# 96 matmuls without use in place of 196, at other places of TensorE's order

## The chip, the cores and the metric

One core of one Trainium2 chip. The metric is the device time of one execution of the whole program, in microseconds (us), as the median over runs. TensorE is written PE in the profile (PEld its weight loads), VectorE DVE, ScalarE ACT, GpSimd POOL and SyncE, which issues all transfers, SP.

## What is computed

Two layers, one after the other. The first is attention over 4 batches, 8 heads, 768 positions and 64 channels a head, in which a query sees only those keys that fall in the same bucket. A bucket is the pattern of signs of six random projections. The second mixes the attention's output x (4 x 768 x 512): an angle per element, a product with two 768 x 768 matrices along the positions, and a product with a 512 x 512 matrix.

```python
mask = q_bucket[:, :, :, None] == k_bucket[:, :, None, :]
scores = np.where(mask, scale * np.matmul(q, k.transpose(0, 1, 3, 2)), -1e9)
attn_out = softmax(scores) @ v
theta = x @ w_theta
y = einsum('ts,bsd->btd', w_tok_r, x * cos(theta)) + einsum('ts,bsd->btd', w_tok_i, x * sin(theta))
u = x + y
out = u + maximum(u @ w_ch, 0)
```

## The kernel before

The attention runs in 96 steps (batch, pair of heads, block of 128 queries, two heads a step). A step's work is a fixed sequence. TensorE makes the scores of 128 queries against 768 keys in PSUM (operation `dst` in batch 0, `st` later; tiles `nat`, `hl`, `kb`, `rows`). VectorE takes their maximum (`mc`, L685, or with the mask added L678). ScalarE takes the exponential (`pf`, L698 or L695) and rounds it to 16 bits (`pp`, L704). GpSimd or VectorE makes the remainder (L711). A transposing transfer turns both (`pt`, issued at L715). TensorE multiplies them with the values (`vv`, eighteen matmuls of 64 or 65 columns). When three blocks are through, VectorE divides by the sum (`x`, L765).

Between these steps stands the other work: weights and values are brought in from 64-bit form (`raw`, `wf_th`, `wf_ch`, L240 to L273 and L328 to L357), and the second layer of a batch whose attention is done runs beside the attention of the next (transposes of x at L815, angles, the products with `wtk`). The last batch's second layer stands alone at the end.

All of it is recorded as some 3,500 operations with their dependences. A table, ORDER, gives the order in which they are issued. Each engine gets its instructions in that order and works through them strictly in order; semaphores make it wait where the table's order needs another engine's result. In the table a number is an operation, a digit behind a colon the buffer that it takes, a letter the engine. An entry f0 to f3 is a matmul without use (L148 and L164 to L171):

```python
if x[0] == "f":
    filler(int(x[1:])).alts["PE"][1]()
    continue
...
def go():
    mm(bank(sl, [P, 4, P], "fill"), idle_, idle_.unsqueeze(1).to_broadcast([P, 4, P]), True, True)
```

It loads the constant tile `idle` (128 x 128, 16 bits) as weights and multiplies 512 columns of it into the PSUM bank that the digit names. Nobody reads the result. In the trace these are `ps<-idle`. PSUM has eight banks; scores take six of them, two at a time, and the rest are the small tiles' (`m`, numbers 0 to 3, of which 2 and 3 alone are in use in the first part). A matmul into a bank waits until the bank's last reader is through. All matmuls go through one helper and have line L96, so they are told apart by their tiles.

Of the kernel before, what the change touches and what calls it, by code (L numbers as in the profile page):

```python
# [990 lines left out]
6:0.1 229:0 f2 1 f3 f2 205:0.0 f3 13:0 f2 238:0 f3 7:1 f2 799:0 f3 34:0 f2 373:1 3 f3 2 5D 796:1 236:2 208 234:3 237:0 0 230:2 235 206 232:3 231 f2 233 f2 f3 f2 207 f3 248:0 14 209 239 210G 247:1  # L991
258:0 267:2 211 259 260 249 261:0 240:0 f2 212G f3 f2 250 241 f3 262:0 251 269:1 242 f2 268:0 181:1.0 252:1 264G 243 28 8 253:1 270 263D f3 f2 254G 271 f3 278 265:0 272:2 288:1 255D 273:2 279 280 9
256:1 281:0 310:2 275G 298:2 244:0 287:0 15 282:3 245 f2 376:2 299 274G 289 17 f3 312:0 283G f3 276:2 11 374:3 300 284G 377:1 301:1 290 19 291 182 285:3 292:2 246 f2 f2 f2 311:1 302:0 29 379:0 184 30
304G 293:1 375 331:0 31 321 303G 20:0 10 257:2.0 313 21 314 f3 294G 322 341:1 266 315:0 305:1 22 f3 295G f3 342 316:2 f3 343 323 350:2 12D 296:0 344:1 317D 324:2 35 330:0 378 36 325:3 351:1 183 327G
38 23 f3 f3 332 f3 514:0 32 f3 326G f3 286 352:2 345:0 f3 318G 306 328:3 185 353 333 297 334 347G 354 335:2 277 186D 319:1 346G f3 16 f3 f3 361 f3 336:1 f3 389:0 348:0 362 355:0 363 337G 307 308 338D
187 18G f3 364:1 f3 399:0 f3 f3 408:2 24 400 401 188D 365:3 25 157:1.0 402:2 367G 388:1 40 410:1 49:1 356:2 409:0 366G 380 26 f3 f3 358G 411 403:0 309 368:2 320:3 412 390 349 413:1 357G 517:2 404G
359:1 329 518:0 33G 41:0 391 381:0 515:2 392 419 393:0 339:0 420 37 421 405D 428:2 382 160 406:3 158 394:3 159 27 422:2 395G 429:1 161 516 55:0 423:2 451:0 519 439:2 396G 414:1 383 340 430 162G f2 360
431 440 42 f2 424G 441 397:0 f2 453:0 442:0 f2 369 425D f2 443:0 f2 50 f2 426:1 f2 432 f2 163 454 f2 444G 455 384 f2 433:2 f2 445D 491:1 51 446:2 456:0 416D 385:1 452:2 4 434:3 387 386 f2 43 f2 f2
471:0 462 164G 520:0 463 415D 435G 133:1.0 464 f2 370 465:1 f2 371 473:1 f2 f2 436G 398:2 52 372 407 417:0 39G 474 44 466:2 472:2 475 493:2 476:2 467G 437:3 494 521 457:0 492:0 468G 53 482 f3 458G f3
655:1 483 447 484 56 485:1 f3 f3 469:2 f3 134 f3 427 486:1 135 f3 522:0 477:3 418 487D 488G 438 523 136 495 502 529:2 478G 489:1 496:1 503 448 57 459G 45 530:1 449 47 504 450 656:3 479G 460:0 505:0  # L1000
540:0 54G 531 497:2 480:3 658:2 58 532 533 541 498G 542 534:2 657:1 524 550:0 659 499D 660 46 543:1 549:2 48 506:1 569:1 544:0 551:1 507G 59 461:3 525 546 f2 508D 481 500:0 137 545 490 535:3 552 553
f2 560 f2 554:0 f2 f2 536 547:3 f2 f2 561 526:0 562 f2 571:2 f2 537 470 563:1 f2 509:1 572 138D f2 f2 f2 555:2 60D f2 501 139 538:2 570:2 557 573 528 574:2 527 575:0 61 592:0 556 661:0 580 577 593:1
# [219 lines left out]
```

## Time and profile before

| | us |
|---|---|
| median of 3 runs | 734.14 |
| lowest and highest | 729.14, 736.46 |
| the profiled execution | 729.0 |
| its span, first to last instruction | 727.2 |
| PE busy in it | 714.3 |
| matmuls without use, busy | 59.6 (196 of 379 ns in the median, which overlap) |
| DVE busy | 588.3 |
| ACT busy | 535.4 |

Busy time of PE is the union of its matmuls' times from issue to the last result, so neighbours overlap: the start of the next tells how long one holds the engine. Stretches are named by us from the span's start.

### The profile page before, as it was taken

How to read it: one execution, taken by the hardware profiler on the slowest of the kernel's cores; microseconds unless marked ns; L12 is line 12 of the kernel's file. 1: busy time of each engine (PE TensorE's matmuls, PEld its weight loads, DVE VectorE, ACT ScalarE, POOL GpSimd, SP SyncE). 2: the span in 40 equal slices, each digit the busy share in tenths (PEclk: the TensorE clock that was granted, in tenths of full speed). 3: DMA queues.
4: the chain of work that ended last, by engine and by line, in shares of the span. 5: the costliest groups of instructions: out<-in, count | busy, mean ns of one | idle time of the engine just before them, and what ended most of it. 6: DMA issues, size and time to landing. Idle time of an engine off the chain costs nothing.

```text
span 727.2 us, 17462 instructions
## 1 busy us (share of the span) xinstructions
PE 714.3 (98%) x6644; PEld 468.2 (64%) x6644; DVE 588.3 (81%) x1343; ACT 535.4 (74%) x718; POOL 430.3 (59%) x461
## 2 busy tenths in 40 slices
PE   8999999999999999999999999999999999999998
PEld 3455555566756566787856676777656676884456
DVE  5879986889999999989888886989997887747223
ACT  3786887979999778778998775778986776756000
POOL 4576576776557776976666767556666666611000
PEclk9999999999999999999999999999999999999999
DMA  8899999997786999999867998997769989940002
GB/s 338 178 213 224 198 184 215 177 239 169 172 180 143 195 216 190 231 195 209 167 113 150 205 169 170 184 209 119 135 125 169 168 169 170 167 95 16 1 0 87
DMA packets 324044, 120.97 MB, mean 166 GB/s; under 512 B 306316, under 2 KB 313848, under 8 KB 323960
## 3 DMA queue, kind: packets, MB, share of 16 engines
q1 hardware_dynamic: 323960, 119.86, 82.1%
q8 instruction: 52, 0.85, 0.5%
q14 instruction: 32, 0.26, 0.1%
HBM read 32.56 MB, written 6.29 MB: 53 GB/s over the span
## 4 chain that ended last, share of the span: by engine, by line
PE 69%; DVE 11%; DMA 8%; ACT 7%; issue 3%; POOL 1%; SPq 0%; DVEq 0%; ACTq 0%; POOLq 0%
PE ps L96 67%; DMA pt<-pp 6%; DVE pf L678 3%; PE ps L815 2%; ACT pp L704 2%; ACT pf L695 2%; DVE mk L674 1%; POOL pp L711 1%; DVE l_x L824 1%; DMA raw<-in_wt_dram 1%; ACT pf L698 1%; DVE f L893 1%; DVE raw L331 1%; DVE vv L404 1%; ACT n L856 1%
## 5 line engine op out<-in xcount | busy, mean ns | idle before, releaser
L711 POOL TENSOR_TENSOR pp<-pf,pp 128x384 f16<-128x384 f32 x372 | 347.1, 957 | 186.5 <-ACT pp L704 141.5
L96 PE MATMUL ps<-z,wtk 128*128 128x512 f16 x864 | 203.2, 379 | 0.4 <-DVE rows L536 0.4
L695 ACT ACTIVATE pf<-pf,mc 128x768 f32<-128x768 f32 x144 | 133.3, 930 | 53.5 <-DVE mc L681 41.5
L704 ACT ACTIVATE pp<-pf 128x768 f16<-128x768 f32 x192 | 159.7, 838 | 15.4 <-DMA pt<-pp 12.9
L678 DVE CUSTOM_DVE_ANT_1 pf<-ps,mk 128x768 f32<-128x768 f32 x144 | 136.6, 952 | 31.7 <-POOL pp L711 15.1
L96 PEld LDWEIGHTS <-pt 128*128 128x128 f16 x3456 | 120.4, 97 | 27.7 <-issue 6.9
L96 PEld LDWEIGHTS <-wtk 128*128 128x128 f16 x864 | 78.6, 98 | 87.4 <-issue 4.0
L96 PE MATMUL ps<-vv,pt 128*128 128x65 f16 (+1 forms) x3456 | 129.5, 193 | 1.0 <-DVE x L933 0.4
L96 PE MATMUL ps<-hl 64*128 64x512 f32 (+1 forms) x864 | 97.7, 352 | 1.3 <-DVE mc L678 1.3
L96 PEld LDWEIGHTS ps<-hl 64*128 64x128 f32 x864 | 73.2, 184 | 27.8 <-issue 9.4
L674 DVE TENSOR_SCALAR mk<-kb,qc 128x768 bf16<-128x768 bf16 x144 | 85.1, 604 | 0.3
L96 PE MATMUL ps<-nat 64*128 64x512 f32 (+1 forms) x192 | 71.0, 506 | 0.3 <-ACT pf L698 0.2
L96 PE MATMUL ps<-wth,h_x 128*128 128x512 f32 x192 | 65.2, 420 | 0.2 <-DVE l_x L824 0.2
L96 PE MATMUL ps<-wch,h_u 128*128 128x512 f32 (+1 forms) x200 | 64.4, 405 | 0.0
L698 ACT ACTIVATE pf<-ps,mc 128x768 f32<-128x768 f32 x48 | 46.9, 985 | 22.5 <-DVE mc L691 16.0
L96 PE MATMUL ps<-idle 128*128 128x512 f16 x196 | 59.6, 391 | 3.4 <-DVE l_x L824 1.2
L904 POOL TENSOR_TENSOR z<-f,z 128x512 f16<-128x512 f32 x25 | 32.3, 1295 | 47.1 <-ACT z L898 34.7
L685 DVE TENSOR_REDUCE mc<-ps 128x1 f32<-128x768 f32 x48 | 45.1, 948 | 11.6 <-PE ps L96 10.5
L820 ACT ACTIVATE h_u<-ps 128x512 fp32r<-128x512 f32 x24 | 14.2, 591 | 50.0 <-PE ps L815 33.8
L96 PEld LDWEIGHTS ps<-nat 64*128 64x128 f32 x192 | 28.8, 186 | 25.9 <-issue 17.9
L893 DVE SCALAR_TENSOR_TENSOR f<-x,zsc,z 128x512 f32<-128x512 f32 x48 | 37.4, 798 | 4.4 <-ACT z L882 2.7
L96 PEld LDWEIGHTS ps<-wch,h_u 128*128 128x128 f32 x200 | 35.7, 188 | 7.8 <-ACT rows L543 0.3
(125 smaller groups left out, 961.5 us busy)
## 6 DMA issues: line engine op xcount, KB each, us to landing
nat<-in_qk_dram SPq DMA_DIRECT2D x32, 384.0 KB, 3.9
raw<-in_wt_dram SPq DMA_DIRECT2D x12, 768.0 KB, 5.1
vb<-in_v_dram SPq DMA_DIRECT2D x16, 384.0 KB, 4.2
out_dram<-x SPq DMA_DIRECT2D x23, 256.0 KB, 2.8
kb<-rows SPq DMA_DIRECT2D x48, 96.0 KB, 2.6
pt<-pp SPq DMA_TRANSPOSE x192, 4.2
w_th<-in_moe_w_theta_dram SPq DMA_DIRECT2D x4, 512.0 KB, 5.5
w_ch<-in_moe_w_ch_dram SPq DMA_DIRECT2D x8, 256.0 KB, 4.0
```

The costliest lines, as they stand in the source:

```text
L96: PE.matmul(out_, l, r, start=start, stop=stop, skip_group_check=True)
L674: DVE.tensor_scalar(u["mk"][:, :, : S // 3], t["code"][:, j].rearrange("p (a n) -> p a n", a=3), t["qc"][:, i, j : j + 1], -APART, ALU.not ...
L678: DVE.tensor_tensor_reduce(u["pf"].rearrange("p (a n) -> p a n", a=3), st[j].rearrange("p (a n) -> p a n", a=3), u["mk"][:, :, : S // 3], ...
L685: DVE.tensor_reduce(col(0), st[j], AX.X, ALU.max, negate=True)
L695: ACT.activation(u["pf"], u["pf"], AF.Exp, bias=col(2), scale=1.0 / math.sqrt(D))
L698: ACT.activation(u["pf"], st[j], AF.Exp, bias=col(2), scale=col(1))
L704: ACT.activation(u["pp"][:, 0], u["pf"], AF.Copy)
L711: return lambda: eng.tensor_tensor(u["pp"][:, 1, cols], u["pf"][:, cols], u["pp"][:, 0, cols], ALU.subtract)
L815: PE.transpose(u["pt"][:, c], src()[:, c * P : (c + 1) * P], ident)
L820: ACT.activation(u["hi"], u["pt"], AF.Copy)
L893: DVE.scalar_tensor_tensor(u["f"], tl[b][:, tt], zsc[:, b : b + 1], t["zw"][r][:, tt], ALU.mult, ALU.mult)
L904: return lambda: eng.tensor_tensor(t["z"][r, 1][:, tt], u["f"], t["z"][r, 0][:, tt], ALU.subtract)
```

## The change

The table alone is changed. Its 3,518 operations stay, with the same order, buffers and engines. Of the 196 f entries 96 are left, and most of these stand elsewhere: 196 in 160 places (a place is a run of f entries without another between), the longest of eight, against 96 in 34 places, the longest of fifteen. By bank f0 to f3 they were 26, 28, 75 and 67, and are 0, 31, 36 and 29. The first ten, in front of the first useful matmul, are the same. By the useful work that they stand beside, with the stretches in which the trace of before has that work:

| stretch, us | 0:9 | 9:62 | 62:75 | 75:150 | 150:224 | 224:260 | 260:727 |
|---|---|---|---|---|---|---|---|
| before | 10 | 41 | 19 | 61 | 52 | 5 | 9 |
| after | 10 | 24 | 2 | 44 | 15 | 1 | 0 |

(One of before lies across 62 us and counts in both columns.) The first line of the table:

```diff
-6:0.1 229:0 f2 1 f3 f2 205:0.0 f3 13:0 f2 238:0 f3 7:1 f2 799:0 f3 34:0 f2 373:1 3 f3 2 5D 796:1 236:2 208 234:3 237:0 0 230:2 235 206 232:3 231 f2 233 f2 f3 f2 207 f3 248:0 14 209 239 210G 247:1
+6:0.1 229:0 f2 1 f3 f2 205:0.0 f3 13:0 f2 238:0 f3 7:1 f2 799:0 f3 34:0 f2 373:1 3 f3 2 5D 796:1 236:2 208 234:3 237:0 0 230:2 235 206 232:3 231 233 207 248:0 14 209 239 210G 247:1 258:0 267:2 211 259
...
```

VectorE's, ScalarE's, GpSimd's and SyncE's instructions stand in the same order as before, with the same waits.

PE, beside the first batch's second block of scores, near 16 us: `row`, `ones` and `vam` belong to the scale of the values, `nat`, `kb` and `rows` to the scores. Before:

```order
L96 LDWEIGHTS row_104
L96 MATMUL ps<-ones,row_104 128x1
L96 LDWEIGHTS idle
L96 MATMUL ps<-idle 128x512
L96 MATMUL ps<-nat_0_116 128x512
L96 LDWEIGHTS rows_88
L96 MATMUL ps<-kb_90,rows_88 128x512
```

After:

```order
L96 LDWEIGHTS idle
L96 MATMUL ps<-idle 128x512
L297 MATMUL ps<-ident,vam_0_170 1x128
L96 LDWEIGHTS row_104
L96 MATMUL ps<-ones,row_104 128x1
L96 MATMUL ps<-nat_0_116 128x512
L96 LDWEIGHTS rows_88
L96 MATMUL ps<-kb_90,rows_88 128x512
```

The matmul without use between `ones` and the scores is gone. A run of three, whose last is shown, stands in front of the transpose of `vam` now; before, a run of four stood behind that transpose.

PE, at the first angles of batch 0, near 153 to 156 us: `ident,x` are transposes of the attention's output, `hl` scores of batch 1, `wth` with `h_x` and `l_x` the angles. Before:

```order
L96 MATMUL ps<-hl_0_1458 128x512 x6
L96 MATMUL ps<-hl_0_1458 128x256 x6
L96 LDWEIGHTS idle
L96 MATMUL ps<-idle 128x512
L96 MATMUL ps<-wth_96,h_x_0_2080 128x512
L96 MATMUL ps<-wth_97,h_x_0_2080 128x512
L96 MATMUL ps<-wth_96,l_x_0_2081 128x512
L815 MATMUL ps<-ident,x_597 128x128 x4
L96 LDWEIGHTS idle
L96 MATMUL ps<-idle 128x512
L815 MATMUL ps<-ident,x_597 128x128 x4
```

After:

```order
L96 MATMUL ps<-hl_0_1420 128x512 x6
L96 MATMUL ps<-hl_0_1420 128x256 x6
L96 MATMUL ps<-wth_96,h_x_0_2024 128x512
L96 MATMUL ps<-wth_97,h_x_0_2024 128x512
L96 MATMUL ps<-wth_96,l_x_0_2025 128x512
L815 MATMUL ps<-ident,x_580 128x128 x8
```

The matmuls without use between the scores, the angles and the transposes are gone, so that two groups of four transposes follow each other at once.

## Rows read from the trace of the kernel before

**Rows 1.** The page: engines' busy time and share; granted clock by slice; the chain by engine.
```profile
PE 714.3 (98%) x6644; PEld 468.2 (64%) x6644; DVE 588.3 (81%) x1343; ACT 535.4 (74%) x718; POOL 430.3 (59%) x461
...
PEclk9999999999999999999999999999999999999999
...
PE 69%; DVE 11%; DMA 8%; ACT 7%; issue 3%; POOL 1%; SPq 0%; DVEq 0%; ACTq 0%; POOLq 0%
```

**Rows 2.** Windows: start and end, length, busy us (and instructions) by engine, clock, DMA.
```profile
9.00:62.00 53.00, 51.92 (x359) 26.31 (x358) 44.38 (x96) 40.66 (x54) 30.56 (x29) 1.00 0.96 235
62.00:75.00 13.00, 13.00 (x119) 7.09 (x115) 12.71 (x33) 8.85 (x11) 8.47 (x9) 1.00 1.02 234
75.00:150.00 75.00, 74.09 (x744) 43.07 (x743) 62.23 (x143) 63.19 (x82) 51.77 (x56) 1.00 0.98 195
150.00:224.00 74.00, 71.32 (x668) 47.13 (x665) 70.38 (x156) 69.76 (x95) 46.30 (x46) 1.00 0.87 184
224.00:260.00 36.00, 35.20 (x332) 20.95 (x334) 32.91 (x80) 28.11 (x44) 27.58 (x32) 1.00 0.91 181
260.00:727.20 467.20, 461.60 (x4420) 320.82 (x4419) 362.57 (x830) 322.81 (x432) 261.29 (x280) 1.00 0.77 146
```

**Rows 3.** Chain that ended last, by line, of 9:62, 75:150, 150:224, 224:260, 260:727 us.
```profile
by line: PE ps L96 94.6%; ACT pf L698 1.9%; DVE kb L495 1.5%; PE ps L297 1.2%; issue 0.8%; DVE ones L301 0.5%; DVE mc L691 0.3%; ACTq L698 0.0%
...
by line: PE ps L96 72.7%; DMA pt<-pp 15.7%; ACT pf L698 5.2%; DVE mc L685 2.6%; issue 2.0%; PE ps L297 1.0%; ACT pp L704 0.9%; DVE ones L301 0.4%; DVE mc L688 0.3%; ACTq L704 0.0%; DVE mc L691 0.0%; POOL pp L711 0.0%; ACTq L698 0.0%; ACTq L
...
by line: PE ps L96 22.4%; DVE pf L678 11.2%; issue 8.0%; DVE mk L674 7.3%; DMA raw<-in_wt_dram 6.9%; DVE f L893 6.0%; DVE z L904 3.9%; DVE l_x L824 3.6%; DVE raw L331 3.0%; DVE raw L328 2.7%; DVE vv L404 2.6%; DVE qt L578 2.5%; DVE x L765 2
...
by line: PE ps L96 47.9%; DMA pt<-pp 16.8%; ACT pf L695 10.1%; ACT pp L704 6.8%; issue 4.5%; ACT hl L449 4.3%; DVE pf L678 2.5%; POOL pp L711 2.4%; DVE x L933 2.1%; ACT wf_ch L249 1.8%; ACT wf_ch L250 0.8%; ACT wch L270 0.5%; DVE mc L678 0.
...
by line: PE ps L96 74.1%; DMA pt<-pp 6.3%; PE ps L815 3.1%; DVE pf L678 2.4%; issue 2.3%; ACT pp L704 2.0%; ACT pf L695 1.6%; POOL pp L711 1.1%; DVE mk L674 0.7%; ACT n L856 0.7%; DVE l_x L824 0.6%; ACT L695 0.5%; ACT h_x L820 0.5%; DVE z L
```

**Rows 4.** Windows of the tile idle alone: the matmuls without use.
```profile
9.00:62.00 53.00, 11.25 (x41) 3.25 (x40) 0.00 (x0) 1.00 0.96 235
62.00:75.00 13.00, 5.03 (x19) 1.46 (x18) 0.00 (x0) 1.00 1.02 234
75.00:150.00 75.00, 17.47 (x61) 4.93 (x62) 0.00 (x0) 1.00 0.98 195
150.00:224.00 74.00, 17.00 (x52) 4.41 (x52) 0.00 (x0) 1.00 0.87 184
224.00:260.00 36.00, 1.56 (x5) 0.42 (x5) 0.00 (x0) 1.00 0.91 181
260.00:727.20 467.20, 3.25 (x9) 0.87 (x9) 0.00 (x0) 1.00 0.77 146
```

**Rows 5.** Timeline of PE near 1, 10 and 64 us: start, length, instruction, idle before.
```profile
1.12 4.07 PE L96 MATMUL ps<-idle 128*128 128x512 f16 x10 [1.12 <-DVE idle L80]
...
9.96 0.81 PE L96 MATMUL ps<-idle 128*128 128x512 f16 x3 [0.27 <-DVE kb L495]
...
63.88 1.89 PE L96 MATMUL ps<-idle 128*128 128x512 f16 x8
```

**Rows 6.** DVE's waits, 9:62 us (three), then 75:150 (two): total, times, longest.
```profile
DVE mc L685 <- PE ps L96: 3.3, 4, 1.8
DVE rows L478 <- PE ps L96: 1.7, 1, 1.7
DVE ones L301 <- PE ps L96: 1.2, 1, 1.2
...
DVE mc L685 <- PE ps L96: 7.2, 8, 2.7
DVE ones L301 <- PE ps L96: 1.4, 1, 1.4
```

**Rows 7.** Timeline of PE near 150 us.
```profile
150.65 0.82 PE L96 MATMUL ps<-idle 128*128 128x512 f16 x3
...
152.72 0.33 PE L815 MATMUL ps<-ident,x 128*128 128x128 f32 x1 [0.92 <-DVE x L765]
```

More of the change, by code (lines that the diff above doesn't have):

```diff
@@ new lines @@
+345:0 318G 306 328:3 185 353 333 297 334 347G 354 335:2 277 186D 319:1 346G 16 361 336:1 f3 f3 f3 f3 389:0 348:0 362 355:0 363 337G 307 308 338D 187 18G 364:1 399:0 f3 f3 408:2 24 400 401 188D 365:3
+25 157:1.0 402:2 367G 388:1 40 410:1 49:1 356:2 f3 f3 f3 409:0 366G 380 26 358G 411 403:0 309 368:2 320:3 412 390 349 413:1 357G 517:2 404G 359:1 329 518:0 33G 41:0 391 381:0 515:2 392 419 393:0 339:0
+420 37 421 405D 428:2 382 160 406:3 158 394:3 159 27 422:2 395G 429:1 161 516 55:0 423:2 451:0 519 439:2 396G 414:1 383 f2 340 430 162G 360 431 440 42 424G 441 397:0 453:0 442:0 369 425D 443:0 50
@@ new lines @@
+568 635 619 636 610:1 637:2 671:1 69 800 621:2 798D 647:3 801G 670:0 666 638:2 66 672:0 640 588 625 681 626:0 639 682 602:3 673 589 627:0 3515:2 3516 70:0 674 590 67 641:0 802:0 675:2 629 683 f1 f1
+622 2572:0.0 667:1 76:1 628 676:1 591 f1 f1 f1 f1 f1 f1 f1 691:0 649 630:3 684:0 677 f1 f1 690:1 648 701:2 678 650:2 642 702 692 668 807:1 693 703 694 2573 704:1 679:0 669 808:0 71 f2 f2 f2 f2 f2
+710:0 685:2 77 815:0 72 803 687 695:2 611 712:1 705:0 631 686 696:3 713 733:1 714 2574 688:1 715:0 78 698 74 809 804 f2 711:0 80 697 735:0 79 707 699:3 651 736 737 721 680:2 738:2 706 82 810:1 722
@@ new lines @@
+716:1 723 81D 734:1 708:2 724:1 717 816 811 812:0 718 725:2 753:0 744 73 727 944:1 83:0 689 745 84 719:0 739:3 746 2575 726 755:2 747:0 805:0 f1 f1 f1 817:0 740 728:1 818 85 756 748:0 754:1 757 86 75D
+758:1 749 806 947:0 773:0 87 764 814 741 89 700 765 766 750 775:1 767:2 709 88 768:1 751:3 f1 f1 774:1 90 759:2 770 776 742:2 720 784 945:1 769 729 652 91:0 946G 730 785 731 819 777 786 771:0 813
+787:0 732 778:2 761 834:0 2579:1 820 2580:0 760 824:1.0 97:1 788:0 2581 779:3 825:1 790 653 2582:0 826:0.1 821:0 789 2589:2 844:1 2599:1 781 827 835:0 2583 828 780 654 2584 948 836 92 2585 782:1
@@ new lines @@
+2590:1 949G 853:0 2586:0 843:1.0 2591 829:1 2587 837 93 743:3 830 2600:0 762:2 845:2.2 772 95 2592:2 831 846 872:1 847 791:0 98 2593 94 2576 99 2594 848:3 2595 823 101 850 752 854:1 963:0 783 100
+1095:1 2588D 822 763 2596:1 103 849 855 2601 856 2597 2602:0 96D 857:2 862:1.0 2598A 863:0 859 838:0 964 858 2639 2603 873:1.2 839 860:3 104:0 874 864:1 792 840 f1 f1 f1 f1 f1 f1 f1 f1 f1 f1 f1 f1 f1
+f1 f1 965:0 851:1 865 793 102G 894:1 2604 794 105 866 2605 795 2640:2 841:2 2609:1 2643:0 106 884:0.1 2641D 2606:1 832:0 107 2642G 867:2 885:0 950:2 2607 2644A 868 2610:1 886:0.0 2629:3 951:1 2645G
@@ new lines @@
+919 2723 934 2636:0 882 883 918 2724 2663A 2637 2725 122 920:0 2659:0 1093:0 972:1.0 2655D 2660A 971 911:1 927:0 893:3 2664D 935 929 124 1111:0 961 902 936:1 2678:0 982:1 928 973:0 2628A 2679 937
+983:0.2 115 930:2 2702 1096 2680 938 974:1 2703 2638A 984 117D 985 2681 1094D 991:0.1 121 2661D 986:2 1240:0 2682 992:1 939:3 2665 987 1001:0 125:0 2704 1112 988 2683 1002:2.0 2726 123G 921 975 1003
+993:2 2684 976 970 1097D 1010:1.0 2669:2 1243:1 2705 2666:1 989:0 977:3 931 2672:0 912 978 126 2673A 1042:0 127 940 2667A 994 1011:1 979 1113:0 2727 2670A 941 2674D 1004 2706 2671G 942 2685 943 1005:0
@@ new lines @@
+1054 154D 1055 1070:1.0 1119 1056:2 166 1063 2745 167 155 1071:0 1057 168 2746 2734 1259:0 1241:1 1028 1058 1109 1064 2747 1072:1.2 156G 1059:1 169 1065:3 2748 1073 1081:1 170G 2749 1074 1118 173:1.2
+1067 1082 1120:1.0 1130:0 1075:0 1049:2 1121:1 1066 1083 2766:2 1076 1131:0.0 171 1068:0 2750 1084:2 1077 1132 2767 1029 1140:0 1244 172G 2751 1122:2 176 1041:1 1086 1123 1149:1 2768 1124 1078:3 174
+2752 175 1125:1 1242D 1139:0.1 1133 189:0.1 1030 1126 1031 1391:0 2753 1260 1134:3 1127 177 1069 1085 1150:2.2 f3 1261:0 2754 1136 1087:0 1141:1 2755 1079 1135 1142 1151 1159:1 1143 1158:1.0 1128:3
@@ new lines @@
+1168:0 178G 1245D 2769 179 192 190 1050 1144:0 2577 180D 1060 191 1152 1262 1146 2770 197:2.0 2756 193 1246:3 1137:2 1169:1.0 1145 1153:2 1088 1247:1 1160:1 1154 1263 1251:0 1388:1 1181:0 1155 2771
+1252 1161 1200:1 1180:0.1 1162 194G 1156:1 1248 198 1163:1 1170 1253 2772 1182:0.2 195 1147:0 1165 2773 1171 199 1129:3 1164 1172:3 1089 2774 1264 1183 1190:0 1254:0 1138 1174 1166:3 1255 1090 1191:1
+2775 1184 1173 2776 1091 1265:1 196D 1249:0 1175:2 1199:0.1 1192 1185:2 1267 200 1186 1193 2788:1 213:1.2 1201:2.0 2789 1256:1 1250 1187 201 1202 2790 1209:0 1194:0 2791 202D 1258 1203 1210:2 1196
@@ new lines @@
+2713:0 1157 1219:1 2714:1 1195 1218:0.1 1211 1204:1 2715 1212 2578 1188:1 1205 1176 1220:1.1 1389:0 2777 1206 1213:3 1257 1197:2 1167 2691:0 214 203 215 2792 2692:0 1228:0 204G 2793 216 1278:1 217
+1214 221:0.1 2794 1221 1229:0 1222 1207:3 1148 1215 1230 1269:0 1223:2 1268:0.1 1177 1178 1231 218D 1216:0 1224 1179 2795 1392 1279:0.2 1225 1232:0 1189:3 1270:1 2796 219 1226:1 1234 2797 1271 222
+1233 1272 1287:1.0 1288:1 1280 1297:0 1273:1 223 1198 1281 1289:2.0 1275 2798 1235:2 2693 1208 1282:3 1274 1217 1316:1 224 1283 2799 225 1407:0 1298:1 2735:0 1276:3 226G 1299 1306:1.0 2778 1300 1284
@@ new lines @@
+1290 2800 227 220G 1301:2 1227 1307:0 1285:0 228D 1291 1236 1303 1317:1.2 2716:2 1292:0 1237 1266 2810:0.0 1302 2694:1 1390G 2695 1338:1 2696 1308:1 2697 1408 1294 1539:1 1328:0.1 1304:1 1238 1293
+1318 1309 2698 1310 1329:0 1409:0 1393G 2717 1319 2699 1330:0.0 2718 1311:1 1410 2719 1331 1239 2736:0 1536:0 1312 1394:1 1295:2 1332 2737 1277:3 1313 2720 1320:3 1399:0 1348:0 2721 1395:0 1322 1339:1
+2757:2 1333:2 1314:3 1305 1321 1400 1357:1 1347:0.1 2758:1 1396 1335 1323:1 1340 2759 1341 2738:1 1334 1401 1358:2.2 1397:2 1342:0 1404:0 1411 1402:0 1286 1398 1349:0 1344 2739 1403 1406 1412 2740
@@ new lines @@
+1523 1532 2887D 2889:2 2888G 2913 1696 1587 1697 2858 1533 2896D 2890A 2933:0 1588:2 2891G 1603:1 2934 1534 2859:0 2935 1596 1590 2860 2936 1535 1578:3 2937 1589 2861D 1698:2 1597:0 1580 1591:1 2955:3
+1604:1.1 1699 2914 2898 1599 1605 2938 1706 2892:2 1693:2 1579 2915 1612:0 2956 2916 1598 1581:3 1613:2 2957 2893A 1606 1614 1624:1.0 2908:0 1600:2 2894D 2897D 2958 2905:2 1707 1832:1 2959 1607:1
+2902:1 2939 1694 1609 1625:1 2903A 2960 1615 2904D 2940 1608 2917 1634:0 1616:2 1626:0.0 2918 2906A 1618 1573:2 1627 1635:1 1592 1617 1610:0 1601 1636 2899:1 1637 2961 2962 1619:1 2900A 1638:3
@@ new lines @@
+2031 3020 3051 2016:3 2039 2130D 2032:3 3065:2 2040 1967 2056:0 2033 2046:0.1 2047:1 2132 2034 2152 2041:1 3057 1948 2023 2057:1.2 3052:1 1976 3066:1 2042 2025:1 3058:3 2058 1977 2069:0 2153:1 2133G
+3059 1978 2048:1 2059 3060 1979 3061 3067 2043 2068:1.0 2078:1 3062:0 2049 2044:2 3053 2060:0 3054D 3075:0 2070:0.0 2061 2017:2.1 3076:0 2035:0 3068:1 2050 3063 2062 3069 2071 2051:2 2079:2 2276:0
+3070 2072 2063:3 2052 3077 3071 2080 2097:0 3085:3 2081 2053 2087:1.0 2088:1 3072:2 2155 3086:1 3078:0 3064D 2073:1 3087 3079 3105 2089:2.1 2075 3088:3 3073 2074 3080 2107:1 3081 3074D 2090 3095:1
@@ new lines @@
+2036 3096:0 3106:1 3089 3082:0 2054:0 3107D 2091 3090 3083 3108G 3097 3091 3112:2 2134:0 3115:0 3113A 2026 2135:1 3084D 2139:1 3114G 2098:0 3116A 2064 2092:3 3109:1 2055 2140 2093 2045 2082:0 2136
+2106:1.0 3092:2 2065 2141 2083 2116:0 3118 2144:1 3110D 2142:0 2094 3098:1 3093 2076:1 3099 2066 2084 2117:1.1 3100 3111G 2108:2 2085:3 3101 3094A 2099 3125:2 2137:3 3117G 2156:0.1 2138 2279:1 2118
+2109 2143 3119:1 2110 2146 3188:3 3166:0 3120D 3167 2067 2119 3122:0 3168 2095:0 3144:2 3121D 3123A 3126D 3189 2111:2 3124G 3127D 3169 2120:1 3145 3102:1 2122 3190 2145 2100 3191 3103 2121 2101:0 3170
```

116 lines of the change are left out of this document (36 added, 80 removed), and 50 rows, old and new, of the table ORDER.

## Prediction

> **What bounds the kernel now.** I read the page's engine shares first. TensorE is busy for 98% of the span, VectorE for 81%, ScalarE for 74%, and the chain that ended last lies on TensorE for 69%; the granted clock is full in every slice [rows 1]. That looks like a kernel bound by TensorE, but part of its busy time is matmuls that nobody reads, so I cut the span into stretches and asked for the engines and for the useless matmuls ("idle" ones from here on) in each.
>
> The table by stretch shows two kinds of time [rows 2]. From 62 to 75 us VectorE is busy 12.71 of 13 us, and from 150 to 224 us 70.38 of 74: there VectorE sets the pace. From 9 to 62 us it is busy 44.38 of 53 and from 75 to 150 us 62.23 of 75, while TensorE is busy 51.92 and 74.09. The chain by stretch agrees: TensorE's matmuls hold 94.6% of it from 9 to 62 us, 72.7% from 75 to 150, only 22.4% from 150 to 224, then 47.9%, and 74.1% (with 3.1% for transposes) from 260 us to the end [rows 3].
>
> The Trainium skill, page Perfetto Trace Analysis, section Identifying the Most-Contended Engine, says that the matmul row's busy share is a poor measure and that for TensorE the weight loads' busy share should be compared with the other engines' occupancy. Loads are busy 64%, VectorE 81% [rows 1], so by that rule VectorE is the contended engine, idle matmuls cost nothing, and the sum would be 0. The chain by stretch speaks against it for two of the early stretches and the long last one [rows 3].
>
> **The change, part by part.** On the other four engines nothing moves, and TensorE's useful matmuls keep their order. What changes is how many idle ones stand before each of them. Their number by stretch is 41, 19, 61, 52, 5 and 9 [rows 4]; in the new order, placed beside the same work, 24, 2, 44, 15, 1 and 0. The first ten, before 9 us, stay.
>
> Price of one: a run of eight lasts 1.89 us and a run of three 0.81, so five more cost 1.08, or 0.216 us each [rows 5]. That is what an in-order engine loses when useful work stands ready behind it. Where useful work would have waited anyway, it costs nothing.
>
> From 9 to 62 us: 41 out, 24 in, 17 fewer at 0.216: 3.7 us. TensorE holds the chain, as at the scores near 16 us, where the idle matmul in front of them goes, so I count all of it. This also takes the 24 that stay at full price, as if none stood in a wait; against that, some waits that idle matmuls fill today come back bare. TensorE's idle time in this stretch is 53 less 51.92, or 1.1 us, and I leave that as it is. Bounds: nothing, if each removed one only uncovers a wait; at best what VectorE waits for TensorE here, for it can't be faster than without those waits: 3.3, 1.7 and 1.2 us in the largest rows, 6.2 in all [rows 6].
>
> From 62 to 75 us: 19 out, 2 in. VectorE has 0.3 us to give, so 0; this is the cover for the 17 removed.
>
> From 75 to 150 us: 61 out, 44 in, 17 fewer: 3.7 us. Bounds: nothing, and the waits of VectorE for TensorE, 7.2 and 1.4, together 8.6 [rows 6].
>
> From 150 to 224 us: 52 out, 15 in, the 15 in a single run before one transpose. 37 at 0.216 would be 8.0 us of TensorE's time, but VectorE is idle for only 3.6 us of the stretch [rows 2]. I count 0, since the chain has TensorE at under a quarter here; at best the 3.6. Those between the scores and the angles near 154 us are among them. What is late next is VectorE itself: one idle run of three ends as the transposes begin, and the last of these waits 0.92 us more for VectorE's result (its multiply at L765) [rows 7]. With the run taken out, that wait is longer by the run and nothing else changes.
>
> From 224 to 260 us: 4 fewer are 0.9 us, of which the chain's share, 47.9%, is 0.4. After 260 us 9 go: 1.9 us, and 77.2% of the chain is TensorE's: 1.5. Bounds: nothing, and 0.9 and 1.9.
>
> Idle matmuls write other banks now. One of those removed waited for its bank: of the run of three at 9.96 us the first stood 0.27 us for VectorE's read of the projected bits [rows 5]. The new ones stand in banks whose last reader is further back in the order, and I expect no such wait: 0, at worst the same 0.27 us in each of the 25 places behind 9 us (6.8 us), at best the same 0.27 gained. Nothing on another engine waits for an idle matmul, so no queue is held up but TensorE's own. The DMA queue's issues keep their order; they come earlier with the work that they wait for.
>
> Sum: 3.7 + 0 + 3.7 + 0 + 0.4 + 1.5 = 9.3 us off the profiled execution's 729.0 us (a span of 727.2 and 1.8 around it), so 719.7. The median of the three runs, 734.1, stands 5.1 above the profiled one; I carry the difference over to it: 724.8 us.
>
> **The clock.** The first ten idle matmuls take 4.07 us, nearly twice the price above [rows 5]: at the start TensorE runs at the lower of its two levels, 1.2 GHz. After that the clock is at 2.4 GHz in every stretch [rows 2], and the engine is never idle long: the whole table has it idle 2.7 us between 150 and 224 us, the stretch where it waits most. No row of before shows the clock falling in the middle, so its price has to be bounded: half speed costs half a microsecond of work per microsecond. The Trainium skill, page TensorE: Matmul & The Clock Gate, section Why this matters for your kernels, says that idle time between bursts of matmuls brings the clock down to half. This trace neither contradicts nor shows that, since its gaps are filled; it speaks against a change that opens them. What it would make of the time is the third rival's price.
>
> **The rivals.**
> First, the same again under another name: the removed matmuls stood where the engine has to wait, so each stretch keeps its length, and only the last two terms remain: 1.9 us, 732.2. For it: ScalarE and VectorE are busy 63 and 62 of 75 us themselves [rows 2], and scores may only start when ScalarE has emptied their banks, so a TensorE that is ahead soon stands. Against it: in two stretches VectorE waits for TensorE, 14.8 us in the rows shown [rows 6]. Anything under 7.3 us, 1% and about what a measurement can tell here, counts in this case.
>
> Second, better than forecast: the 68 idle matmuls left between 9 and 62 and between 75 and 150 us stand in real waits and cost nothing. Then the two stretches give all that VectorE waits for, 14.8, and the end 1.9: 16.7 us, 717.4. Against it: other waits of VectorE's (for ScalarE, for a transfer) come up long before the last of these is gone.
>
> Third, slower: the clock falls between 150 and 224 us, where the new order has one run of 15 and nothing else in place of 52 spread out. TensorE's useful work there is 71.3 less 11.2 (52 at 0.216), 60.1, with the 15 63.3 us, so it has 10.7 us to spare. Each microsecond at half speed takes half a microsecond of that. It decides from 40 of the 74 us on: 20 us lost, 10.7 spare and 9.3 gained elsewhere. At 57 us it loses 28.5, and the kernel ends 8.5 us late: 742.6. For it: the bare gap at the transposes alone is 0.92 us and the run of three before it [rows 7], and there are many like it. Against it: an engine at half speed has no gaps left, and at the start it took steady work to bring the clock up, so it should come back.
>
> That the change does not do what it says can only mean that the waits it was placed by are not those of this chip; then the first rival's time holds.
>
> **How the numbers follow.** Forecast, faster by 7.3 to 14 us: 0.36. Second rival: 0.16. So faster by over 1%: 0.52. First rival, within 1%: 0.33. Third, slower by over 1%: 0.15. Time: 724.8. The range starts at 715, which takes in the second rival, and ends at 738, short of the third rival's price; together about 2 in 10 lie outside.
>
> **What would show it.** Right: idle matmuls number 96; VectorE's waits for TensorE between 9 and 150 us fall to about half; the work that now starts at 150 us starts some 7 us earlier, and the work of 224 us keeps that lead without adding to it; the granted clock stays full. First rival: TensorE's idle time before 150 us grows by as much as the idle matmuls shrink. Third: the clock row falls below full between 150 and 260 us. The forecast is wrong if the lead at 150 us is under 4 us, if the stretch with VectorE at its limit gets shorter by more than 3.6, or if the lead is lost after 260 us.

## The result and the profile after

The changed kernel takes 735.35 us in the median of 22 runs (730.84 to 742.27), the kernel before, beside it, 730.45 (22 runs): a ratio of 1.0055, with an interval of 1.0041 to 1.0069. It is half a per cent slower, where 724.8 us and 9.3 us off had been predicted. Its profiled execution takes 734.41 us, 5.4 more than the one of before (729.0).

The page of the kernel after, busy time by engine and granted clock by slice:

```profile
PE 708.5 (97%) x6544; PEld 466.1 (64%) x6544; DVE 588.0 (80%) x1343; ACT 535.4 (73%) x718; POOL 427.6 (58%) x461
...
PEclk9999899999999999999999999999999999999999
```

TensorE is busy 5.8 us less than before [rows 1], and still the span is 5.4 us longer. One slice of the clock row is below full: 73 to 92 us. Windows of the kernel after, with the columns of [rows 2] (start and end, length, busy us by engine, granted clock, DMA):

```profile
9.00:62.00 53.00, 51.84 (x385) 27.25 (x385) 48.75 (x110) 43.53 (x58) 32.27 (x33) 1.00 1.02 254
62.00:75.00 13.00, 11.04 (x62) 5.16 (x61) 12.72 (x28) 9.08 (x13) 8.06 (x7) 0.82 0.95 214
75.00:150.00 75.00, 71.53 (x668) 41.56 (x668) 54.85 (x131) 56.73 (x74) 46.19 (x50) 0.96 0.89 180
150.00:224.00 74.00, 66.37 (x605) 45.00 (x603) 68.27 (x149) 67.75 (x91) 44.88 (x45) 0.95 0.82 179
224.00:260.00 36.00, 35.55 (x354) 21.62 (x352) 33.69 (x82) 31.45 (x49) 26.81 (x29) 1.00 0.85 176
```

By 62 us VectorE has done 4.4 us more work than before (48.75 against 44.38). From 62 us on the mean clock is 0.82, 0.96 and 0.95, and between 75 and 150 us VectorE, ScalarE and GpSimd all do 5 to 8 us less than in [rows 2]. Something between 62 and 150 us takes away what the first stretch won.

VectorE's waits for TensorE in the kernel after, 9 to 62 us (two rows), then 75 to 150 us, as in [rows 6]:

```profile
DVE rows L478 <- PE ps L96: 1.8, 1, 1.8
DVE mc L685 <- PE ps L96: 0.5, 1, 0.5
...
DVE mc L685 <- PE ps L96: 8.1, 7, 3.3
DVE ones L301 <- PE ps L297: 3.6, 3, 2.6
DVE rc L755 <- PE ps L96: 1.7, 2, 1.3
DVE ones L301 <- PE ps L96: 1.4, 1, 1.4
```

From 9 to 62 us the 6.2 us of waits have become 2.3. From 75 to 150 us they have grown: the two rows named before make 9.5 us in place of 8.6, the row for L297, 0.9 us before, makes 3.6, and the row at L755 is new.

The place where the first gain turns into a loss is in TensorE's timeline near 70 us. First the kernel after, then before (start, length, instruction, idle before in brackets):

```profile
66.09 1.27 PE L96 MATMUL ps<-vv,pt 128*128 128x65 f16 x36
69.31 1.20 PE L96 MATMUL ps<-nat 64*128 64x512 f32 x2 [1.96 <-ACT pf L698]
...
84.55 2.79 PE L96 MATMUL ps<-nat,pjs 128*56 128x512 f32 x8
```

```profile
71.25 1.04 PE L96 MATMUL ps<-idle 128*128 128x512 f16 x4
72.12 1.25 PE L96 MATMUL ps<-vv,pt 128*128 128x65 f16 x36
73.31 1.12 PE L96 MATMUL ps<-nat 64*128 64x512 f32 x2
...
83.87 2.79 PE L96 MATMUL ps<-nat,pjs 128*56 128x512 f32 x8
```

The same thirty-six matmuls start 6.0 us earlier (66.09 against 72.12), the scores behind them 4.0 earlier (69.31 against 73.31): they stand idle for 1.96 us until ScalarE's exponential has emptied their banks. At the next landmark, the product `nat,pjs`, the kernel after is 0.7 us late (84.55 against 83.87). So 4.7 us go in these 15. Windows of the kernel after, around that wait and at a later fall of the clock:

```profile
67.36:69.31 1.95, 0.00 (x0) 0.00 (x0) 1.92 (x6) 1.04 (x2) 1.95 (x2) 1.00 0.97 330
69.31:70.24 0.93, 0.93 (x2) 0.39 (x3) 0.86 (x5) 0.93 (x2) 0.07 (x1) 1.00 1.10 348
70.24:80.48 10.24, 10.24 (x85) 6.43 (x84) 6.80 (x16) 7.34 (x11) 7.41 (x8) 0.50 0.69 165
80.48:90.00 9.52, 9.52 (x39) 4.38 (x36) 7.09 (x16) 6.05 (x8) 1.49 (x2) 1.00 0.80 150
172.64:176.05 3.41, 3.41 (x16) 2.41 (x15) 3.19 (x6) 3.38 (x5) 2.71 (x4) 0.50 0.11 39
```

TensorE does nothing from 67.36 to 69.31 us, works on, and 0.93 us later its clock falls to the lower level, 1.2 GHz, for 10.24 us. It is busy throughout them, so they hold 5.1 us of work at 2.4 GHz, and 5.1 us are lost, close to the 4.7 above. The clock falls again for 3.41 us at 172.64 us, behind 2.36 us in which the angles wait for VectorE, and for 3.41 at 217.01, behind 1.48 us. It did not fall behind every such wait: the transposes near 154 us now wait 2.12 us, and the clock stays full.

```profile
156.67 0.33 PE L815 MATMUL ps<-ident,x 128*128 128x128 f32 x1 [2.12 <-DVE x L765]
```

From here on a kernel's lead is how much earlier the same instruction of VectorE ends than in before's profile, or of TensorE where rows of TensorE are shown. VectorE's instructions stand in the same order in every kernel here, so they are matched by their place in it, and a lead "at 108 us" is that of the instruction that ends at 108 us in before's profile. Some expectations below name leads that differ from these, by almost 3 us near 91 us and by up to about 1 us elsewhere. Before's profile is of one of its faster executions (729.0 us against a median of 730.45), so the leads are on the low side.

In the kernel after the lead is +3.7 us from 60 to 79 us, -0.7 from 85 to 97, -3.2 at 108, -4.4 at 126, -3.7 at 174, -5.9 at 180 and -5.4 at the end. The first drop is that of the clock at 70 us. Part of the second stands near 103 us. Timeline of the kernel after, then of before:

```profile
103.16 0.27 PE L297 MATMUL ps<-ident,wmx 128*1 128x128 f32 x1
103.27 1.89 PE L96 MATMUL ps<-idle 128*128 128x512 f16 x8
105.00 0.71 PE L96 MATMUL ps<-vv,pt 128*128 128x65 f16 x18
```

```profile
101.05 0.27 PE L297 MATMUL ps<-ident,wmx 128*1 128x128 f32 x1
101.28 0.72 PE L96 MATMUL ps<-vv,pt 128*128 128x65 f16 x18
```

A new run of eight idle matmuls stands before eighteen matmuls, which in before start at once. TensorE's lag of 2.1 us becomes 3.7. The third drop, from -2.8 us at 120 to -4.4 at 126, comes at a run of seven. The fourth, 2.2 us at 178, stands behind the run of fifteen. TensorE's timeline of the kernel after, then of before:

```profile
176.10 0.71 PE L96 MATMUL ps<-vv,pt 128*128 128x65 f16 x18
176.66 3.40 PE L96 MATMUL ps<-idle 128*128 128x512 f16 x15
179.89 0.27 PE L297 MATMUL ps<-ident,vam 128*1 128x128 f32 x1
```

```profile
172.61 0.71 PE L96 MATMUL ps<-vv,pt 128*128 128x65 f16 x18
173.16 0.27 PE L297 MATMUL ps<-ident,vam 128*1 128x128 f32 x1
```

TensorE's lag of 3.5 us ahead of the fifteen is 6.7 behind them. VectorE's next read of a product from behind them (L219), in the kernel after, then in before:

```profile
183.41 0.16 DVE L219 TENSOR_SCALAR winv<-ps 128x1 f32<-128x1 f32 x1 [2.79 <-PE ps L96]
```

```profile
177.54 0.16 DVE L219 TENSOR_SCALAR winv<-ps 128x1 f32<-128x1 f32 x1 [0.62 <-PE ps L96]
```

VectorE waits 2.79 us there in place of 0.62, which is the whole drop of 2.2. The two falls of the clock in this stretch cost next to nothing: across the one at 172.64 us the lead goes from -3.5 to -3.7, and across the one at 217.01 it stays at -5.4.

### The profile page after: what moved, and what is told of

Read it like the earlier page. It is cut to its first block, busy times and chain, and to the rows that moved or that the text cites. A ratio compares the mean times of both kernels' runs of the same rounds, so it can differ in the third digit from the quotient of the medians.

```text
span 732.6 us, 17267 instructions
## 1 busy us (share of the span) xinstructions
PE 708.5 (97%) x6544; PEld 466.1 (64%) x6544; DVE 588.0 (80%) x1343; ACT 535.4 (73%) x718; POOL 427.6 (58%) x461
## 5 line engine op out<-in xcount | busy, mean ns | idle before, releaser
L96 PEld LDWEIGHTS <-wtk 128*128 128x128 f16 x864 | 78.5, 98 | 88.1 <-issue 5.5
L96 PE MATMUL ps<-hl 64*128 64x512 f32 (+1 forms) x864 | 100.6, 356 | 2.9 <-DVE mc L678 2.8
L96 PEld LDWEIGHTS ps<-hl 64*128 64x128 f32 x864 | 75.2, 187 | 29.8 <-issue 8.9
L96 PE MATMUL ps<-nat 64*128 64x512 f32 (+1 forms) x192 | 77.4, 517 | 2.8 <-ACT pf L698 2.7
L96 PEld LDWEIGHTS ps<-nat 64*128 64x128 f32 x192 | 31.2, 190 | 32.1 <-issue 17.6
L96 PE MATMUL ps<-wth,l_x 128*128 128x512 f32 x96 | 38.4, 400 | 2.4 <-DVE l_x L824 2.4
```

What stands on the lines that cost most here:

```text
L96: PE.matmul(out_, l, r, start=start, stop=stop, skip_group_check=True)
```

## The experiments

All are the table alone. In the diffs only the part of a line around an edit stands. "Clock" is the granted clock over a whole execution; a fall of 10.24 us makes it 0.993, and one of 3.41 us 0.998.

**First: the nineteen of 62 to 75 us put back (after with before's idle matmuls there, 113 in all).**

```diff
-397:0 453:0 442:0 369 425D 443:0 50 426:1 432 163 454 444G
+397:0 f2 453:0 442:0 f2 369 425D f2 443:0 f2 50 f2 426:1 f2 432 f2 163 454 f2 444G
...
```

> The changed order with the 19 idle matmuls of before put back between 62 and 75 us (113 in all). Theory A (the clock's fall at 70 us, 10.2 us at half speed, took some 5 us): no fall there, the lead of about 4 us at 62 us is still there at 85 us, time some 4.7 us under the changed kernel, near 730.7. Theory B (removal buys nothing, the lead would be lost to other waits and to idle matmuls in front of ready work): lead gone by 108 us either way, time near 735.

Measured: 736.72 us, ratio 1.0056 (1.0026 to 1.0086). The fall at 70 us is gone, and the lead is +3.3 us from 85 to 97 us, where the kernel after has -0.7. But the kernel is no faster, against the first theory's 730.7: the lead runs into the next wait. Timeline of this kernel, then its windows from there on:

```profile
90.91 0.81 PE L96 MATMUL ps<-idle 128*128 128x512 f16 x3
93.33 0.72 PE L96 MATMUL ps<-vv,pt 128*128 128x65 f16 x18 [1.61 <-DMA pt<-pp]
```

```profile
94.36:108.01 13.65, 13.65 (x47) 5.83 (x46) 3.24 (x5) 4.55 (x6) 7.10 (x9) 0.50 0.57 119
```

It waits 1.61 us for a transfer, and the clock is at 1.2 GHz for 13.65 us after it. The lead is +3.3 us at 97, -5.9 at 103 and -5.7 at 108. In this execution the fall had only moved to the next place where a lead ends in a bare wait.

**Second: the fifty-two of 150 to 224 us put back (133).** The run of fifteen goes, and the scattered ones return.

```diff
-864:1 792 840 f1 f1 f1 f1 f1 f1 f1 f1 f1 f1 f1 f1 f1 f1 f1 965:0 851:1 865 793
+864:1 792 840 965:0 f2 851:1 865 f1 793
...
```

> The changed order with the 52 idle matmuls of before in place of the 15 between 150 and 224 us (133 in all). Theory A: the fall at 70 us stays, the two of 3.4 us at 172 and 217 us go, time 1.5 to 3.4 us under the changed kernel, 732 to 734. Theory B: VectorE sets the pace there, so no difference, 735.

Measured: 732.87 us, ratio 1.0012 (0.9989 to 1.0034). In its profile the fall at 70.24 us is still there (10.24 us), the two at 172 and 217 are gone, and the lead is -4.1 at 174 and at 180 us, where the kernel after drops from -3.7 to -5.9; VectorE's wait at L219 is 0.63 us. By the ratios (1.0055 less 1.0012) the late stretch of the change costs 0.43%, or 3.1 us. This run takes the fifteen and the two falls away together; that it is the fifteen, for 2.2 us of it, is read from the profile of the kernel after.

**Third: the new places of 9 to 62 us alone, all else as before (180).**

```diff
-270 263D f3 f2 254G 271 f3 278 265:0 272:2 288:1 255D 273:2 279 280 9 256:1 281:0 310:2
+270 263D 254G 271 278 265:0 272:2 288:1 255D 273:2 279 280 9 256:1 281:0 f2 f2 f2 f2 f2 310:2
...
```

> The order of before with the new 24 in place of 40 idle matmuls between 9 and 62 us, all others as before (180 in all). Theory A: the clock stays full, the 3.7 us of lead that the changed kernel has at 62 us are kept to the end, time 3 to 4 us under before, near 727. Theory B: the lead at 62 us is the same 3.7, but is absorbed by 150 us, time as before, near 730.5.

Measured: 730.06 us, ratio 0.9981 (0.9958 to 1.0005). The lead is +3.9 us at 60 and still +3.3 at 132: the term of the first stretch, to within half a microsecond. Then it goes at once. Timeline and window of this kernel:

```profile
130.85 1.87 PE L96 MATMUL ps<-nat 64*128 64x512 f32 x2 [1.80 <-ACT pf L698]
```

```profile
131.09:137.92 6.83, 6.83 (x47) 3.52 (x46) 3.31 (x6) 4.85 (x8) 4.98 (x5) 0.50 0.56 113
```

The scores stand 1.80 us for ScalarE, the clock falls 0.24 us later, and the lead at 139 us is -1.6. By time the ten executions do not differ by their clock: six with 0.998 or more have a mean of 730.8 us, four with 0.995 to 0.997 have 730.5.

**Fourth: both of the first two together (150).** The edit is the two diffs above.

> The changed order with the idle matmuls of before between 62 and 75 us (19) and between 150 and 224 us (52), 150 in all. Theory A: clock full everywhere, time 6 to 8 us under the changed kernel, 727 to 729, under before. Theory B: near 735, or 733 if the falls cost something.

Measured: 731.66 us, ratio 0.9998 (0.9974 to 1.0023). Up to 94 us its profile is that of the first experiment, down to the wait:

```profile
93.35 0.72 PE L96 MATMUL ps<-vv,pt 128*128 128x65 f16 x18 [1.60 <-DMA pt<-pp]
```

```profile
94.36:108.01 13.65, 13.59 (x119) 7.50 (x118) 8.79 (x25) 9.43 (x12) 9.21 (x12) 1.00 0.92 185
```

Yet the clock doesn't fall: 119 matmuls in the 13.65 us that held 47. So the wait alone does not decide, and one kernel's executions differ. Of this kernel's ten, six have a clock of 0.998 or more and a mean of 730.7 us, four have 0.993 and 734.8: in this kernel a fall goes with 4.1 us. In the profiles the fall is worth more: at 103 us the lead is +0.6 here and -5.9 in the first experiment. With the clock full the lead is still lost, though later: +3.3 at 97 us, +0.6 at 103, +1.2 at 120, -0.4 at 126. At these two places the runs of eight and of seven stand, which the change brought.

**Fifth: the third, with eight idle matmuls in the wait near 130 us (188).** The eight write into a bank that a small product is in (f3), so that this product's value is changed.

```diff
-78 698 74 809 804 711:0 80 697 735:0 f2 f1 79
+78 698 74 809 804 f3 f3 f3 f3 f3 f3 f3 f3 711:0 80 697 735:0 f2 f1 79
```

> e3 with eight idle matmuls more in front of the scores at 129 us, where TensorE stood bare for 1.8 us before the clock fell (188 in all). If the bare wait is what lets the clock fall: clock full, the lead of 3.3 us shrinks at that wait to some 1.5 to 2 (ScalarE's time there) but isn't lost, time 1 to 2 us under before, 729. If the fall comes from something else: it stays at 131 us, with 5 us lost as in e3, 730.

Measured: 729.50 us, ratio 0.9979 (0.9961 to 0.9996). The scores follow the eight at 131.44 us, and the same window is at full clock:

```profile
129.61 1.90 PE L96 MATMUL ps<-idle 128*128 128x512 f16 x8
131.44 1.12 PE L96 MATMUL ps<-nat 64*128 64x512 f32 x2
```

```profile
131.09:137.92 6.83, 6.83 (x60) 3.70 (x58) 3.85 (x8) 6.83 (x13) 5.31 (x7) 1.00 0.98 202
```

All ten executions have 0.998 or more, against six of ten without the eight. But the time is the same (0.9979 against 0.9981): the lead of +2.7 us at 132 is +1.0 at 139 and -0.9 at 168. The eight are more than the wait needs, since the scores start 0.6 us later than in the third (131.44 against 130.85). ScalarE is busy for all 6.83 us of that window; here the lead is spent on the other engines, whatever the clock. The first rival, that a lead is absorbed, is right for this version.

**Sixth: the fourth without the runs of eight and of seven (135).**

```diff
-576 62:0 f2 f2 f2 f2 f2 f2 f2 f2 510 603
+576 62:0 510 603
...
-676:1 591 f1 f1 f1 f1 f1 f1 f1 691:0 649
+676:1 591 691:0 649
```

> e4 without the run of eight idle matmuls at 103 us and the run of seven near 121 us (135 in all). If these two stand in front of work that is ready: the lead of 4.2 us at 102 us is kept to 115 us in place of 1.0, and time is 2 to 3 us under e4, 728 to 729. If they stand in waits: the lead is the same 1 us at 108 us, with bare waits there and perhaps a fall of the clock, 731.7 or more.

Measured: 730.48 us, ratio 0.9964 (0.9932 to 0.9996), and wide: 725.93 to 737.17. Five executions with a clock of 0.998 or more have a mean of 727.4 us, 3.3 less than the fourth's six at that clock (before's own means at that clock, beside the two, differ by 0.2): that is what the two runs cost. Three with 0.993 have 731.7, and two with 0.986 took 734.25 and 737.17. The profiled one, of 0.993, has a fall of 10.24 us at 95.27, again behind the wait for the transfer (1.64 us).

**Seventh: before without its last fourteen (after 224 us, with the single one of the change; 183).**

```diff
-1047 f0 2712 f0 2744:0 1110
+1047 2712 2744:0 1110
...
```

> The order of before without the last 14 idle matmuls but the one of the changed order near 257 us (183 in all). By the terms of the prediction 0.4 and 1.5: 1.9 us under before, 728.5 to 729.5. If the work behind most of them waited anyway: no difference, 731.

Measured: 732.09 us, ratio 1.0003 (0.9980 to 1.0027). The lead stays within 1 us of zero up to 600 us and is -1.5 at the end. No gain is to be seen: the 1.9 us of the two terms would be 0.9974, below the interval.

**Eighth: only the first ten left (10).**

```diff
-231 f2 233 f2 f3 f2 207 f3 248:0
+231 233 207 248:0
...
```

> No idle matmul but the first ten. If bare waits let the clock fall: several falls between 20 and 260 us, more time at half speed than the 17 us of the changed kernel, time over 737. If the idle matmuls only cost: 5 to 10 us under before, 722 to 726.

Measured: 745.37 us, ratio 1.0148 (1.0084 to 1.0213). The page's clock row of this kernel:

```profile
PEclk9679889568999999999999999999999999999999
```

Eight falls, 78.5 us before 232 us. The first, at 16.42 us, comes behind idle times of only 0.59 and 0.37 us. The lead at the end is -19.2.

**Ninth: the sixth, with the run of three near 91 us made ten (142).**

```diff
-138D 555:2 60D f2 f2 f2 501 139
+138D 555:2 60D f2 f2 f2 f2 f2 f2 f2 f2 f2 f2 501 139
```

> e6 with the run of three idle matmuls near 91 us made ten (142 in all), so that the bare wait of 1.6 us behind it, after which the clock fell in e6, is filled. If the fall took the lead (6.0 us at 91 us, -2.2 at 108): clock full, the lead is about 4 us at 97 us and still 3 to 4 at 108, time 3 to 4 us under before, 727 to 728. If not: the lead at 108 us is 0 or less and time is that of before.

Measured: 727.62 us, ratio 0.9934 (0.9911 to 0.9957): below both kernels. Five of six executions have 0.998 or more (727.4 us). The ten now fill the wait for the transfer:

```profile
90.85 2.32 PE L96 MATMUL ps<-idle 128*128 128x512 f16 x10
93.30 0.72 PE L96 MATMUL ps<-vv,pt 128*128 128x65 f16 x18
```

The eighteen start at 93.30 us with the ten as at 93.51 with three. The profiled execution, the sixth, took 734.12: its clock fell later, behind a bare wait of 0.89 us, and its lead went from +2.2 at 134 us to -3.5 at 142.

```profile
132.00:145.65 13.65, 13.28 (x80) 7.44 (x79) 6.24 (x16) 8.74 (x13) 8.09 (x10) 0.50 0.72 147
```

**Tenth: before with the run of eight of 103 us added (204).**

```diff
-576 f2 62:0 510 603
+576 f2 62:0 f2 f2 f2 f2 f2 f2 f2 f2 510 603
```

> The order of before with one run of eight idle matmuls added where the changed order has its run of eight, in front of a product with the values near 101 us (204 in all). If that product is ready there: TensorE is 8 times 0.216, 1.7 us late at once, and up to 1.7 us of it reach the end: 732 to 733.5 beside 731.5. If it waits there: nothing, 731.5.

Measured: 733.99 us, ratio 1.0027 (1.0007 to 1.0047); the clock of the profiled execution is full. Its timeline, to be read beside the two at 103 us above:

```profile
101.26 0.27 PE L297 MATMUL ps<-ident,wmx 128*1 128x128 f32 x1
101.37 1.89 PE L96 MATMUL ps<-idle 128*128 128x512 f16 x8
103.09 0.71 PE L96 MATMUL ps<-vv,pt 128*128 128x65 f16 x18
```

The eighteen start 1.8 us later than in before. Of these 1.3 arrive (lead -0.2, then -1.5 at 108 us), and they stay to the end. (The table of before has no run of more than three; where TensorE's timeline of before shows eight in a row, entries of other engines stand between them.) The run stands before ready work.

**Eleventh: the ninth, with the one near 130 us made five (146).**

```diff
-78 698 74 809 804 f2 711:0 80 697
+78 698 74 809 804 f2 f2 f2 f2 f2 711:0 80 697
```

> The last kernel (142 matmuls without use, 0.9934 of before), with the single one that stands before the scores near 130 us made a run of five. In its profile these scores stood bare for 0.89 us (130.31 to 131.21 us, for ScalarE's pf at L698), and the clock fell to half at 132.00 us for 13.65 us, over which the lead on before's VectorE work went from +2.6 us to -2.5. Theory (the clock is lost behind such bare waits, and idle matmuls that fill one keep it): no fall between 130 and 150 us, a lead of +2 to +3 us kept past 145 us, the profile near 728 us, and the median at or a little below the last kernel's, ratio 0.990 to 0.994, because its undisturbed runs were already near 726. Rival (falls come with the execution and not with the bare wait): the fall stands there again or at another place without a bare wait ahead of it, and the ratio stays 0.993 to 0.997. Second rival (the four more stand in front of ready work): clock full, lead at 135 us smaller by 0.9, ratio 0.994 to 0.997.

Measured: 728.30 us (726.40 to 730.29), ratio 0.9938 (0.9913 to 0.9963). All twelve executions have a clock of 0.998 or more. The wait at 130 us is filled, and the window of the ninth's fall is at full clock:

```profile
129.29 1.25 PE L96 MATMUL ps<-idle 128*128 128x512 f16 x5
130.57 1.12 PE L96 MATMUL ps<-nat 64*128 64x512 f32 x2
```

```profile
130.00:145.00 15.00, 14.21 (x134) 7.84 (x132) 11.82 (x27) 14.27 (x21) 11.12 (x12) 1.00 1.04 185
```

The lead is +2.2 us at 139 and at 180, +3.0 at 260 and +1.0 at the end. It is not faster than the ninth, whose executions at that clock were as fast (727.4 us against 728.5); what went is the spread.

## Why the prediction was wrong

The result lies within 1% of before, the case that had 0.33, but not for the reason of the first rival: a gain was made and more than given back. That 735 us still lies inside the range of 715 to 738 is luck: one gain of 3.7 us came, the other terms did not, and the losses, which are not in the sum at all, happened to be small beside the range. The steps together, as ratios to before: the change 1.0055; with the late stretch put back 1.0012; with 62 to 75 us put back as well 0.9998; without the two runs 0.9964; with the wait for the transfer filled 0.9934. The intervals of the first two ratios do not meet; those of later neighbours overlap, but the second ratio and the last are clearly apart, and so are the third and the last.

**9 to 62 us, 3.7 us: right.** The lead is 3.7 us at 60 to 79 us in the kernel after and 3.9 at 60 in the third experiment. In time it does not arrive alone: the third experiment's interval reaches past 1. The other places and banks brought no wait that shows. The rule cited from the Trainium skill, page Perfetto Trace Analysis, section Identifying the Most-Contended Engine, by which idle matmuls cost nothing here, would make this lead 0; the trace does not agree with it in this stretch.

**62 to 75 us, 0 us: the step that failed first.** It read "VectorE has 0.3 us to give, so 0; this is the cover for the 17 removed". VectorE's pace does hide them: VectorE is busy 12.72 of 13 us, as before, and its lead does not grow. But the step priced an idle matmul only by the time it takes, not by the clock that it keeps. Behind the 1.96 us of bare wait TensorE ran 10.24 us at half speed, into the next stretch, where VectorE waits for it: the lead goes from +3.7 to -0.7, more than the gain of the stretch before. With the nineteen put back it is +3.3 there (first and fourth experiment). That alone makes the kernel no faster, as the first experiment shows: in five of its ten executions the clock is still 0.988 or less.

**The third rival had a fall of the clock, at the wrong place and with the wrong price.** It let the clock fall only between 150 and 224 us. There it falls twice, for 6.8 us in all, and that is hidden, as the rival's 10.7 us of TensorE's time to spare would have it: 0.2 us of lead and 0. Where TensorE holds the chain there is nothing to spare, and a single fall is enough: 4.4 us of lead for 10.24 us at half speed at 70 us, and 6.5 for 13.65 us at 94 (first experiment against the fourth). The Trainium skill, page TensorE: Matmul & The Clock Gate, section Why this matters for your kernels, says that idle time between bursts brings the clock down; the trace of the kernel after agrees that falls follow idle time, with 1.48 to 2.36 us ahead of its three falls, which is shorter than what the section warns of, and shows none behind two others, of 1.67 and 2.12 us. The rival's chance of 0.15 was for over 1% slower, which did not come; but the remark that the engine is never idle long, on which the clock was taken as full, came from a trace whose gaps were filled.

**75 to 150 us, 3.7 us: not there.** At full clock the lead is 3.9 us at 72 us, up to 4.7 at 83 and 3.3 at 97 (fourth experiment), and 3.7, 4.6 and 3.6 in the eleventh; at 150 us the eleventh, in which neither a fall nor the two runs take any, has 2.2. So the seventeen fewer gave nothing that lasts. VectorE's 8.6 us of waits for TensorE were no proof that it waited for idle matmuls. And the two runs were counted as 15 of the 44 that stay, but they stand in front of ready work: 1.3 us for the one alone (tenth), 3.3 for both by the executions of 0.998 or more (sixth against fourth).

**150 to 224 us, 0 us:** right that nothing is won, wrong that nothing is lost. The fifteen that were left stand in front of a product that VectorE needs next, and cost 2.2 us of lead, although VectorE is busy 70.38 of 74 us in before. The term took a stretch's busy share as cover for a run at one place. That the wait at the transposes near 154 us would grow "and nothing else changes" is right: it is 2.12 us in place of 0.92, and the lead across it stays at -4.0.

**224 us to the end, 0.4 and 1.5 us: not there.** The seventh experiment took them alone, 1.0003. The chain's share of TensorE, 77%, said who ends last, not that these nine stood before ready work.

The signs named in advance: VectorE's waits for TensorE fell to less than half from 9 to 62 us but grew from 75 to 150; the lead at 150 us is -3.8, under the 4 us that were to make the forecast wrong, and the clock row is below full, though the slice lies before 150 us.

What stays open: why the same wait brings a fall in one execution and none in another. The first and the fourth experiment are alike up to 94 us. In the twelve profiles (the eighth experiment's apart) TensorE waits bare for 1.4 us or more 17 times; nine of these waits are followed by a fall within 1.8 us, eight are not. So such a wait alone does not decide it. Open is also why the lead shrinks by 1.2 us between 97 and 108 us even with the wait filled (eleventh), and how the 3.1 us of the late stretch divide beyond the fifteen. Before's own executions are not all at full clock either: of 90 taken beside the experiments, 64 have 0.998 or more (731.5 us in the mean), 22 have 0.994 to 0.998 (733.2).

## What to carry to other kernels

An idle matmul has two prices: its 0.216 us where ready work stands behind it, and, where it is taken out of a wait, the half-speed time that may follow. The busy share of another engine over a stretch does not tell that either is covered: with VectorE at its limit two falls cost 0.2 us of lead, and one run of fifteen cost 2.2, because what VectorE needed next stood behind it. Idle matmuls belong where useful work waits in the kernel that is to run, not in the one that was traced: each gain moves the waits, so profile again after each move, look at every bare wait that the lead has made longer, and fill it. And count the clock over many executions, since one profile shows only whether that execution fell.

## What was not expected of the hardware

- The clock fell behind waits as short as 0.89 us (ninth experiment) and, with hardly any idle matmuls, behind 0.59 and 0.37 us (eighth), and did not fall behind 1.60 us (fourth) or 2.12 us (the kernel after). The falls last 3.4 to 17.1 us in these profiles, though TensorE is busy all through most of them.
- The delay between the end of the wait and the fall differs: 0.93 us in the kernel after, 0.24 in the third experiment, 1.0 in the first.
